# Top-k attention and two mixtures of experts on one core: the first replacement of the top-k search writes another buffer, and four smaller moves around it

## The chip, the cores and the metric

The kernel runs on one core of one Trainium2 chip. The metric is the device time of one execution in microseconds; given is the median of three runs. One more execution was taken with the hardware profiler, and all rows of a trace below are from that one. TensorE (PE) multiplies, PEld is its loading of weights; VectorE is DVE, ScalarE is ACT, GpSimd is POOL, and SyncE (SP) issues the DMAs.

## The reference, cut to what matters

```python
# attention: 4 batches, 8 heads, 576 tokens, 64 wide
scores = scale * np.matmul(q, k.transpose(0, 1, 3, 2))
kth = np.partition(scores, -32, axis=-1)[..., -32:-31]
scores = np.where(scores >= kth, scores, -1e9)
attn = np.exp(scores - np.max(scores, axis=-1, keepdims=True))
attn = attn / (np.sum(attn, axis=-1, keepdims=True) + 1e-09)
x = np.matmul(attn, v)                      # then [2304, 512]
# first MoE: w1, w2 [512, 1024], w3 [1024, 1024], w_out [1024, 512]
x = ((x @ w1) * (x @ w2)) @ w3 @ w_out
# second MoE: 8 experts, [512, 1024] and [1024, 512], a gate normalized 8 times
out = sum(P[:, e:e + 1] * (np.maximum(x @ m1[e], 0) @ m2[e]) for e in range(8))
```

## The kernel before

The first stage is a loop over 72 attention steps (and six more that drain it). A step holds two tiles of 128 query rows by 576 keys, `s_sb[st]` (128 x 2 x 576). The work of a step is spread over three turns of the loop. In turn s, VectorE searches the 32nd largest score of step s (`st_topk`), ScalarE marks and exponentiates step s−1 (`st_over`, `st_exp`), GpSimd scales step s−2 by the reciprocal of its sums (`st_norm`), TensorE transposes step s−2 (`st_trans`) and multiplies it with v (`st_av`), and TensorE already makes the scores of step s+1 (`st_scores`), which ScalarE evicts (L203).

The search: VectorE takes the larger of each pair of scores, half against half (`top`, L231). GpSimd has added the halves (`low`, L223) and subtracts `top` from that (L236), so `low` holds the smaller ones. In `rounds`, VectorE finds the eight largest (L242, MAX8) and overwrites them (L248, a MATCH_VALUE_LOAD and a MATCH_REPLACE8), four rounds in `top` and two in `low`, each for both tiles. Then L254 and L255 merge them. `head` is called between the first two maxima and issues the reciprocal (L282, VectorE), the two marks (L261, ScalarE), nbias (L266, GpSimd) and the two scalings (L288, GpSimd); GpSimd's L236 stand behind these in its queue.

Beside this, steps 0 to 23 convert four weights. A 'cv' takes a slab of 128 x 512 words of eight bytes (`raw`, L352), casts its parts with three instructions of ScalarE (L380, L381, L383, the last one in place), clamps on VectorE (`c1`, L390) and adds on GpSimd (L393, or L396 and then a split into two halves, L363 and L364). `c1` waits in the list `dve_q`; `rounds` takes one entry from it at every `dve_slot()`, that is behind each pair of maxima and each pair of replacements. `run_cv` starts at most two cvs a step. `cv_next` issues the load of a later cv. w3's slabs are transposed (L460), copied to `w3t` (L461) and multiplied with w_out into `W` (L469, L471). w1 and w2 are kept as two halves each. From step 24 on, `run_fill` places the products of the first MoE (L510, L528) between the attention's, a budget per step, so that a batch is done by a given step.

The order on every engine is the order in which this code is written; nothing is reordered later. Behind the loop come the rest of the last batch and the second MoE.

Of the kernel before, what the change touches and what calls it, by code (L numbers as in the profile page):

```python
# [18 lines left out]
def kernel(  # L19
# [163 lines left out]
    tkv, nbias, rden = {}, {}, {}  # L183
    eps = const.tile([128, 1], F32, name="eps")
    nc.gpsimd.memset(eps, 1e-9)

    def st_scores(st, j):
        p, h, t = steps1[st][j]
        ps = aps.tile([128, 2, 512], F32, name="sps", tag="sps")
        qs = qst_t[p % 2]  # L190
        if h is None:
            terms = [(qs[:, 2 * S4 + 128 * hh:2 * S4 + 128 * hh + 128], hh, part)
                     for part in range(2) for hh in range(2)]
        else:
            c0 = S4 * h + 128 * t
            terms = [(qs[:, c0:c0 + 128], h, part) for part in range(2)]
        for n, (lhs, hh, part) in enumerate(terms):
# [106 lines left out]
    def st_av(st):  # L304
# [6 lines left out]
        if steps1[st][0][1] is None:  # L311
# [8 lines left out]
            for j in range(2):  # L320
                b, hp = divmod(steps1[st][j][0], HP)
                nc.scalar.activation(xT[b][:, hp, S4:S], ps[:, 64 * j:64 * j + 64], AF.Copy)
            return
# [19 lines left out]
    gsc = G.rearrange("p f t -> p (f t)")  # L343
    cbias = const.tile([128, 2], F32, name="cbias")
    nc.gpsimd.memset(cbias[:, 0:1], -8.0 * 16 * 896)
    nc.gpsimd.memset(cbias[:, 1:2], -8.0 * (16 * 896 + 32768 - 4096))
    nc.gpsimd.memset(gsc[:, 0:2 * CW], 0.0)

    def cv_load(key, src):
        t = cv["p"].tile([128, 4 * CW + 4], U16, name="raw", tag="raw",  # L350
                         bufs=RB - 1 if "w2" in m1p else RB)
        nc.sync.dma_start(t[:, 1:4 * CW + 1], src.bitcast(U16))  # L352
        raws[key] = t

    def cv_next(pos):
        n = pos + (RB if pos < NCA else RB - 1)
        if n < len(cvs) and not pos < NCA <= n:
            cvs[n][1]()
# [11 lines left out]
    def cv_run(key, dst, done=None):  # L370
# [8 lines left out]
        cb = cv["p"].tile([128, CW], F32, name="cb", tag="cb", bufs=2)  # L379
        nc.scalar.activation(ca, y, AF.Relu, bias=cbias[:, 0:1], scale=8.0)  # L380
        nc.scalar.activation(cb, y, AF.Identity, bias=cbias[:, 1:2], scale=8.0)  # L381
        low = rest.bitcast(I32)
        nc.scalar.activation(low, rest, AF.Copy, scale=2.0 ** -13)  # L383

        def split():
            hi_lo(rest.bitcast(F32), *dst())
            cv_next(pos)

        def c1():
            nc.vector.scalar_tensor_tensor(Q.bitcast(U16).rearrange("p (n f) -> p n f", f=2)[:, :, 1],  # L390
                                           ca, 32768.0, cb, op0=ALU.min, op1=ALU.max)
            if key[0] in ("o", "3"):
                nc.gpsimd.tensor_tensor(dst().bitcast(I32), Q.bitcast(I32), low, ALU.add)  # L393
                cv_next(pos)
            else:
# [4 lines left out]

        dve_q.append(c1)

# [52 lines left out]
    def w_trans(i, hf):  # L455
        if hf == 0:
            w3t[i] = wtp.tile([128, FC, 128], F32, name="w3t", tag="w3t", bufs=1)
# [3 lines left out]
        nc.scalar.activation(w3t[i][:, 4 * hf:4 * hf + 4].rearrange("p a b -> p (a b)"), pt, AF.Copy)  # L461
        w3done.add((i, hf))
# [3 lines left out]
    def w_mm(i, j):  # L466
        if j == 0:
            wps[i] = mps.tile([128, 512], F32, name="wps", tag="mm")
        nc.tensor.matmul(wps[i], w3t[i][:, j], wo[:, j], start=(j == 0), stop=(j == FC - 1))  # L469
        if j == FC - 1:  # L470
            nc.scalar.activation(W[:, i], wps.pop(i), AF.Copy)  # L471

    def w_items(i, hf):
        return [(430, lambda: w_trans(i, hf))] + [(860, lambda j=j: w_mm(i, j)) for j in range(4 * hf, 4 * hf + 4)]

# [98 lines left out]
    def run_cv():  # L574
        n = cpos[0]
        if n >= len(cvs) or len(dve_q) > 1:
            return
# [3 lines left out]
        if n == NCA and "w2" not in m1p:  # L581
            if dve_q or cv_post or fill or later_q or (FC - 1, 1) not in w3done:
                return
            wt_close()
            for i in range(RB - 1):
                cvs[n + i][1]()
# [9 lines left out]
    cvs[0][1]()  # L596
    nc.scalar.activation(eps, eps, AF.Copy)
    prep_split(0, "k", nc.vector)
# [10 lines left out]
    cvs[1][1]()  # L609
    cvs[2][1]()  # L610
    load_v(1)
# [21 lines left out]
    for s in range(NS + 6):  # L633
        for fn in loads.get(s, []):
            fn()
        now[0] = s
        if s >= marks[0] and "p" not in m1p and cpos[0] == len(cvs) and not dve_q and not cv_post:
            moe1_pool()
# [45 lines left out]
        if old:  # L684
            st_trans(s - 2, 1)
        if 0 < s and cpos[0] < len(cvs):
            run_cv()
        cv_flush()
        some_prep(1)
# [376 lines left out]
```

## Time and profile before

| | us |
|---|---|
| three runs | 2574.52, 2576.54, 2577.63 |
| median | 2576.54 |
| the profiled execution | 2578.23 |
| its span, from the first to the last instruction | 2576.5 |
| TensorE busy in it | 2328.4 (90%) |
| VectorE busy | 1889.8 (73%) |
| GpSimd busy | 1568.2 (61%) |
| ScalarE busy | 1278.3 (50%) |

The shares are averages over stages with different limits, so they do not tell what a change in one stage is worth; the busy times by stretch do. A time in a row is microseconds from the span's start. Square brackets behind a row hold the idle time of that engine just before it and what ended it. The clock is the one granted to TensorE, as a share of its full speed. An engine's idle time costs something only where another one waits for it.

### The profile page before, as it was taken

To read this page: it belongs to the slowest core of one execution; us is meant where nothing else is said; L and a number is where in the kernel's file an instruction comes from. 1 tells how busy PE (TensorE), PEld (TensorE's weight loads), DVE (VectorE), ACT (ScalarE), POOL (GpSimd) and SP (SyncE) were. 2 spreads that over 40 slices of the span, in tenths; PEclk is the share of its full clock that TensorE was granted. 3 is DMA by queue.
4 is the path that set the end of the run, shared out by engine and by line. 5 is a ranking of instruction groups with operands and counts; after the bars stand their busy time and mean duration, and the time that the engine had idled before them with its cause. 6 is when DMAs were issued, how large, how long until landed. Compare 5 with 4: busy or idle time off the path is not lost.

```text
span 2576.5 us, 38951 instructions
## 1 busy us (share of the span) xinstructions
PE 2328.4 (90%) x13061; PEld 2028.4 (79%) x13061; DVE 1889.8 (73%) x4352; ACT 1278.3 (50%) x2757; POOL 1568.2 (61%) x1657
## 2 busy tenths in 40 slices
PE   4577669978878889999999999999999999999999
PEld 3444458867767768788999998888888899999998
DVE  6756777878777743688777777877777777777776
ACT  6667667666666643344444344434434444434432
POOL 5555666555655431568666667766666666666664
PEclk7788769999989999999999999999999999999999
DMA  4322211111111012322222223222222232222222
GB/s 128 102 71 81 64 53 33 38 38 35 29 41 30 8 40 73 98 70 78 66 66 71 69 66 107 72 68 66 66 66 69 71 91 66 69 72 66 66 66 58
DMA packets 173305, 166.66 MB, mean 65 GB/s; under 512 B 19632, under 2 KB 137392, under 8 KB 173104
## 3 DMA queue, kind: packets, MB, share of 16 engines
q1 hardware_dynamic: 173104, 164.17, 21.6%
q8 instruction: 103, 1.69, 0.3%
q14 instruction: 98, 0.80, 0.1%
HBM read 145.24 MB, written 9.44 MB: 60 GB/s over the span
## 4 chain that ended last, share of the span: by engine, by line
PE 61%; DVE 20%; POOL 7%; ACT 5%; issue 2%; DMA 2%; SPq 0%; POOLq 0%; ACTq 0%; DVEq 0%
PE y L953 29%; PE l1ps L886 25%; DVE tkv L242 8%; DVE top L248 4%; POOL low L236 3%; POOL e_sb L288 3%; PE abps L510 2%; DVE low L248 2%; PE x2ps L528 2%; DVE top L231 1%; DMA raw<-in_moe_w_dram 1%; PE wps L469 1%; ACT e_sb L273 1%; ACT G L380 1%; ACT s_sb L203 1%
## 5 line engine op out<-in xcount | busy, mean ns | idle before, releaser
L750 POOL TENSOR_TENSOR wal<-ws,wah 128x256 fp32r<-128x256 f32 x665 | 555.5, 843 | 480.5 <-ACT wah L749 471.0
L966 DVE SCALAR_TENSOR_TENSOR acc<-y,P,acc 128x512 f32<-128x512 f32 x540 | 402.6, 746 | 219.7 <-PE y L953 218.8
L749 ACT ACTIVATE wah<-ws 128x256 fp32r<-128x256 f32 x672 | 276.4, 413 | 525.9 <-PE l1ps L886 519.0
L953 PE MATMUL y<-wbh,hh 128*128 128x512 f32 x1152 | 457.1, 397 | 4.9 <-ACT hh L907 4.8
L953 PE MATMUL y<-wbl,hh 128*128 128x512 f32 x1152 | 455.2, 395 | 0.0
L953 PE MATMUL y<-wbh,hl 128*128 128x512 f32 x1152 | 449.7, 390 | 1.1 <-DVE hl L910 0.6
L743 DVE TENSOR_TENSOR ws<-ws 128x256 f32<-128x256 f32 x384 | 314.1, 819 | 3.9 <-DMA ws<-in_moe_w_dram 2.7
L886 PE MATMUL l1ps<-xo0h,wah 128*128 128x384 f32 x896 | 304.2, 340 | 0.0
L886 PE MATMUL l1ps<-xo0h,wal 128*128 128x384 f32 x896 | 302.5, 338 | 0.0
L886 PE MATMUL l1ps<-xo0l,wah 128*128 128x384 f32 x896 | 302.3, 337 | 0.0
L953 PEld LDWEIGHTS y<-wbl,hh 128*128 128x128 f32 x1152 | 216.5, 188 | 52.8
L907 ACT ACTIVATE hh<-u 128x384 fp32r<-128x384 f32 x192 | 100.9, 525 | 295.6 <-DVE u L899 295.6
L953 PEld LDWEIGHTS y<-wbh,hh 128*128 128x128 f32 x1152 | 216.9, 188 | 29.9 <-ACT hh L907 7.2
L758 POOL TENSOR_TENSOR wbl<-ws,wbh 128x1024 fp32r<-128x1024 f32 x96 | 232.0, 2416 | 12.6 <-ACT wbh L757 4.6
L953 PEld LDWEIGHTS y<-wbh,hl 128*128 128x128 f32 x1152 | 217.0, 188 | 28.4 <-DVE hl L910 3.9
L242 DVE MAX8 tkv<-top 128x8 f32<-128x288 f32 x576 | 237.9, 447 | 0.0
L294 PE MATMUL tps<-ident,e_sb 128*128 128x128 f32 x576 | 107.7, 318 | 122.6 <-POOL e_sb L288 113.2
L294 PEld LDWEIGHTS tps<-ident,e_sb 128*128 128x128 f32 x576 | 77.7, 163 | 161.6 <-POOL e_sb L288 131.0
L248 DVE MATCH_REPLACE8 top<-tkv,top 128x288 f32<-128x288 f32 x432 | 189.2, 443 | 0.0
L199 PE MATMUL sps<-kst,qst 128*128 128x288 f32 x640 | 143.9, 358 | 47.4 <-ACT s_sb L203 46.7
L886 PEld LDWEIGHTS l1ps<-xo0l,wah 128*128 128x128 f32 x896 | 169.1, 189 | 16.4
L886 PEld LDWEIGHTS l1ps<-xo0h,wah 128*128 128x128 f32 x896 | 168.7, 188 | 15.8 <-DVE u L899 0.6
(148 smaller groups left out, 5311.4 us busy)
## 6 DMA issues: line engine op xcount, KB each, us to landing
ws<-in_moe_w_dram SPq DMA_DIRECT2D x384, 128.0 KB, 2.4
ws<-in_moe_w_dram SPq DMA_DIRECT2D x96, 512.0 KB, 3.5
raw<-in_moe_w_dram SPq DMA_DIRECT2D x32, 512.0 KB, 4.0
kst<-kst SPq DMA_DIRECT2D x30, 288.0 KB, 4.1
xr<-x2s SPq DMA_DIRECT2D x12, 384.0 KB, 3.7
xr<-x2s SPq DMA_DIRECT2D x6, 768.0 KB, 4.6
kn<-in_k_dram SPq DMA_DIRECT2D x16, 256.0 KB, 2.9
qn<-in_q_dram SPq DMA_DIRECT2D x16, 256.0 KB, 2.9
```

What stands on the lines that cost most here:

```text
L199: nc.tensor.matmul(ps[:, e, 0:SH], lhs, kst[p, part][:, hh, SH * e:SH * e + SH], start=(n == 0), stop=(n == len(terms) - 1))
L242: nc.vector.max(vt[:, j, c0 + 8 * r:c0 + 8 * r + 8], x[:, j])
L248: nc.vector.match_replace(x[:, j], vt[:, j, c0 + 8 * r:c0 + 8 * r + 8], x[:, j], -3.0e38)
L294: nc.tensor.transpose(ps[:, 128 * c:128 * c + 128], e[:, 128 * c:128 * c + 128], ident)
L743: nc.vector.tensor_tensor(st[:, dst], st[:, x], st[:, y], op)
L749: nc.scalar.activation(hi, st[:, slot], AF.Copy)
L750: eng.tensor_tensor(lo, st[:, slot], hi.bitcast(F32), ALU.subtract)
L758: nc.gpsimd.tensor_tensor(lo, st, hi.bitcast(F32), ALU.subtract)
L886: nc.tensor.matmul(ps[:, 0:TH], lhs[:, c], rhs[:, slot, c], start=(k_ == 0), stop=(k_ == 3 * KH - 1))
L907: nc.scalar.activation(t["hh"][:, i, h], src, AF.Relu)
L953: nc.tensor.matmul(ps, lhs[:, m, h, o:o + 128], rhs[:, m], start=(k_ == 0), stop=(k_ == 5))
L966: nc.vector.scalar_tensor_tensor(a, ps, P[:, t, e:e + 1], a, op0=ALU.mult, op1=ALU.add)
```

## The change

Five things are done.

1. `st_topk` has a second tile, `rest`. The first pair of replacements reads `top` and writes `rest`; all later rounds of that search work in `rest`. `top` is no longer written after L231 (L230 in the new numbering).
2. `e_sb` is `s_sb`: the exponentials overwrite the scores. `s_sb` has four buffers in place of three, `e_sb`'s two are gone. The sum's 1e-9 is added by VectorE just ahead of the reciprocal, and no longer by ScalarE (L276).
3. The third cast writes to words of its own, to a part of G or to the tile `lw` in turn; `raw` is then free behind the three casts, two of them are kept (three before), and `cv_next` is called right there. `c1` is put into `dve_q` behind two empty entries.
4. The eviction of x (L331, L322) is put off to the next turn of the loop, behind the first exponential.
5. The four products of a half of w3 are put off until the next half has been transposed; `w3t` is two half tiles.

```diff
-            s_sb[st] = ap1.tile([128, 2, S], F32, name="s_sb", tag="s_sb", bufs=3)
+            s_sb[st] = ap1.tile([128, 2, S], F32, name="s_sb", tag="s_sb", bufs=4)
...
+        rest = ap1.tile([128, 2, SH], F32, name="rest", tag="rest", bufs=1)
...
-        def rounds(x, c0, k):
+        def rounds(x, c0, k, y=None):
...
-                        nc.vector.match_replace(x[:, j], vt[:, j, c0 + 8 * r:c0 + 8 * r + 8], x[:, j], -3.0e38)
+                        nc.vector.match_replace((x if y is None else y)[:, j], vt[:, j, c0 + 8 * r:c0 + 8 * r + 8],
+                                                x[:, j], -3.0e38)
+                    x = x if y is None else y
...
-        rounds(top, 0, TOPK // 8)
+        rounds(top, 0, TOPK // 8, rest)
...
-            e_sb[st] = ap1.tile([128, 2, S], F32, name="e_sb", tag="e_sb", bufs=2)
+            e_sb[st] = s_sb[st]
...
-            nc.scalar.activation(rd, rd, AF.Identity, bias=eps)
...
+        nc.vector.tensor_scalar(rd, rd, 1e-9, None, op0=ALU.add)
         nc.vector.reciprocal(rd, rd)
...
-        nc.scalar.activation(xT[b][:, hp, 128 * t:128 * t + 128], ps[:, 0:128], AF.Copy)
+        xev.append(lambda: nc.scalar.activation(xT[b][:, hp, 128 * t:128 * t + 128], ps[:, 0:128], AF.Copy))
...
-    RB = 3
+    RB = 2
...
-        nc.scalar.activation(cb, y, AF.Identity, bias=cbias[:, 1:2], scale=8.0)
-        low = rest.bitcast(I32)
+        low = (cv["p"].tile([128, CW], F32, name="lw", tag="lw", bufs=1) if n else gsc[:, 4 * CW:5 * CW]).bitcast(I32)
+        nc.scalar.activation(ca, y, AF.Relu, bias=cbias, scale=8.0)
+        nc.scalar.activation(cb, y, AF.Copy, bias=-8.0 * (16 * 896 + 32768 - 4096), scale=8.0)
         nc.scalar.activation(low, rest, AF.Copy, scale=2.0 ** -13)
+        cv_next(pos)
...
-        dve_q.append(c1)
+        dve_q.extend([None, None, c1])
...
+        r = [(430, lambda: w_trans(i, hf))] + w_last
+        w_last[:] = [(860, lambda j=j: w_mm(i, j)) for j in range(4 * hf, 4 * hf + 4)]
...
             st_exp(s - 1, 0)
+        st_out()
```

The order on VectorE in one of the steps with two cvs, before: `top` is the tile of the larger scores, `tkv` the maxima found, L390 the clamp of a cv.

```order
L231 TENSOR_TENSOR top<-s_sb 128x288 x2
L242 MAX tkv<-top 128x8
L282 RECIPROCAL rden<-rden 128x2
L242 MAX tkv<-top 128x8
L390 SCALAR_TENSOR_TENSOR G<-G,cb 128x512
L248 MATCH_REPLACE top<-tkv,top 128x288 x2
L390 SCALAR_TENSOR_TENSOR G<-G,cb 128x512
L242 MAX tkv<-top 128x8 x2
L248 MATCH_REPLACE top<-tkv,top 128x288 x2
```

And the same place of the changed program (the clamp is L397 there):

```order
L230 TENSOR_TENSOR top<-s_sb 128x288 x2
L241 MAX tkv<-top 128x8
L282 TENSOR_SCALAR rden<-rden 128x2
L283 RECIPROCAL rden<-rden 128x2
L241 MAX tkv<-top 128x8
L247 MATCH_REPLACE rest<-tkv,top 128x288 x2
L241 MAX tkv<-rest 128x8 x2
L397 SCALAR_TENSOR_TENSOR G<-G,cb 128x512
L247 MATCH_REPLACE rest<-tkv,rest 128x288 x2
L241 MAX tkv<-rest 128x8 x2
L247 MATCH_REPLACE rest<-tkv,rest 128x288 x2
L397 SCALAR_TENSOR_TENSOR G<-G,cb 128x512
```

The first replacement no longer writes what it reads; the two clamps moved from the first and second slot of the step to the third and sixth; one small instruction stands ahead of the reciprocal.

On ScalarE, the end of such a step and the start of the next, before: L297 evicts transposes, three casts of a cv, w3's copy, x, three casts of the second cv, and then the next step's marks and scores.

```order
L297 ACTIVATE et<-tps 128x640
L380 ACTIVATE G<-raw,cbias 128x512
L381 ACTIVATE cb<-raw,cbias 128x512
L383 ACTIVATE raw<-raw 128x512
L461 ACTIVATE w3t<-pt 128x512
L331 ACTIVATE xT<-xps 128x128
L380 ACTIVATE G<-raw,cbias 128x512
L381 ACTIVATE cb<-raw,cbias 128x512
L383 ACTIVATE raw<-raw 128x512
L261 ACTIVATE s_sb<-s_sb,tkv 128x576 x2
L203 ACTIVATE s_sb<-sps 128x576
```

And the same place of the changed program:

```order
L388 ACTIVATE G<-raw,cbias 128x512
L389 ACTIVATE cb<-raw 128x512
L390 ACTIVATE lw<-raw 128x512
L476 ACTIVATE W<-wps 128x512
L466 ACTIVATE w3t<-pt 128x512
L388 ACTIVATE G<-raw,cbias 128x512
L389 ACTIVATE cb<-raw 128x512
L390 ACTIVATE G<-raw 128x512
L262 ACTIVATE s_sb<-s_sb,tkv 128x576 x2
L201 ACTIVATE s_sb<-sps 128x576
L274 ACTIVATE s_sb,rden<-s_sb,nbias 128x576
L333 ACTIVATE xT<-xps 128x128
```

The eviction of x moved from ahead of the second cv's casts to behind the next step's first exponential, and the third cast writes `lw` or G in place of `raw`.

## Rows read from the trace of the kernel before

**Rows 1.** Stretches: from:to, length; busy PE, PEld, DVE, ACT, POOL; clock, DMA share, GB/s
```profile
14.13:81.70 67.57, 31.84 (x178) 26.22 (x178) 54.87 (x173) 50.54 (x96) 42.58 (x45) 0.67 0.44 132
81.70:280.24 198.54, 142.31 (x741) 88.93 (x741) 130.31 (x421) 134.50 (x266) 109.38 (x121) 0.83 0.25 76
280.24:374.97 94.73, 53.78 (x312) 43.27 (x313) 74.28 (x241) 65.31 (x129) 61.24 (x68) 0.68 0.22 67
374.97:526.35 151.38, 138.28 (x1099) 121.98 (x1097) 120.14 (x431) 100.90 (x226) 87.73 (x114) 1.00 0.14 38
526.35:934.20 407.85, 336.24 (x2543) 295.78 (x2543) 323.79 (x1157) 257.61 (x563) 222.21 (x293) 0.93 0.10 27
934.20:2576.40 1642.20, 1620.82 (x8169) 1447.87 (x8169) 1183.77 (x1932) 664.25 (x1470) 1042.47 (x1002) 1.00 0.24 72
```

**Rows 2.** Waits of VectorE in stretches A to E: us in total, times, longest
```profile
DVE top L248 <- POOL low L236: 5.4, 8, 1.4
DVE G L390 <- ACT cb L381: 5.0, 2, 4.8
...
DVE top L248 <- POOL low L236: 38.2, 24, 5.3
DVE G L390 <- ACT cb L381: 23.2, 12, 4.6
...
DVE top L248 <- POOL low L236: 12.7, 11, 2.8
DVE G L390 <- ACT cb L381: 7.2, 4, 2.7
...
DVE top L248 <- POOL low L236: 30.4, 26, 2.4
...
DVE top L248 <- POOL low L236: 81.3, 70, 2.4
```

**Rows 3.** Timeline of step 52, VectorE and GpSimd: start, length, engine, line, instruction
```profile
700.68 0.82 DVE L231 TENSOR_TENSOR top<-s_sb 128x288 f32<-128x288 f32 x2
...
700.84 0.34 POOL L266 TENSOR_TENSOR nbias<-tkv 128x2 f32<-128x2 f32 x1 [4.04 <-DVE tkv L255]
...
701.78 0.15 DVE L282 RECIPROCAL rden<-rden 128x2 f32<-128x2 f32 x1
701.85 0.44 DVE L242 MAX8 tkv<-top 128x8 f32<-128x288 f32 x1
702.10 1.47 POOL L288 TENSOR_SCALAR e_sb<-e_sb,rden 128x576 f32<-128x576 f32 x2 [0.92 <-DVE rden L282]
...
703.54 1.56 POOL L236 TENSOR_TENSOR low<-low,top 128x288 int32<-128x288 int32 x2
...
704.37 0.09 DVE L248 MATCH_VALUE_LOAD top<-tkv,top 128x8 f32 x1 [2.09 <-POOL low L236]
...
705.57 0.81 DVE L242 MAX8 tkv<-top 128x8 f32<-128x288 f32 x2
...
709.44 0.80 DVE L242 MAX8 tkv<-low 128x8 f32<-128x288 f32 x2
...
712.19 0.45 DVE L231 TENSOR_TENSOR top<-s_sb 128x288 f32<-128x288 f32 x1
```

**Rows 4.** Waits: TensorE and ScalarE in stretch B, then TensorE in E
```profile
PE wps L469 <- ACT w3t L461: 41.9, 15, 7.0
...
ACT xT L331 <- PE xps L327: 20.1, 5, 5.7
ACT G L380 <- DMA raw<-in_moe_w_dram: 15.4, 4, 4.6
...
PE tps L294 <- POOL e_sb L288: 64.3, 33, 4.9
```

**Rows 5.** Durations in ns, min/median/max: the clamp, and a small tensor_scalar
```profile
L390 DVE SCALAR_TENSOR_TENSOR G<-G,cb x40: 710/754/1615, 18.0 to 354.4; 128x512 uint16<-128x512 f32 x40
...
L859 DVE TENSOR_SCALAR cs<-cs x8: 171/373/2044, 1073.8 to 1130.0; 128x8 f32<-128x8 f32 x8
```

More of the change, by code (lines that the diff above doesn't have):

```diff
@@ L183 @@
     tkv, nbias, rden = {}, {}, {}
-    eps = const.tile([128, 1], F32, name="eps")
-    nc.gpsimd.memset(eps, 1e-9)
     def st_scores(st, j):
@@ L321, in st_av @@
                 b, hp = divmod(steps1[st][j][0], HP)
-                nc.scalar.activation(xT[b][:, hp, S4:S], ps[:, 64 * j:64 * j + 64], AF.Copy)
+                xev.append(lambda b=b, hp=hp, j=j: nc.scalar.activation(xT[b][:, hp, S4:S], ps[:, 64 * j:64 * j + 64],
+                                                                        AF.Copy))
             return
@@ L330, in st_av, with st_out @@
         b, hp = divmod(p, HP)
-        nc.scalar.activation(xT[b][:, hp, 128 * t:128 * t + 128], ps[:, 0:128], AF.Copy)
+        xev.append(lambda: nc.scalar.activation(xT[b][:, hp, 128 * t:128 * t + 128], ps[:, 0:128], AF.Copy))
+    xev = []
+    def st_out():
+        while xev:
+            xev.pop(0)()
     CW = 512
-    RB = 3
+    RB = 2
     wt = ExitStack()
@@ L343 @@
     gsc = G.rearrange("p f t -> p (f t)")
-    cbias = const.tile([128, 2], F32, name="cbias")
-    nc.gpsimd.memset(cbias[:, 0:1], -8.0 * 16 * 896)
-    nc.gpsimd.memset(cbias[:, 1:2], -8.0 * (16 * 896 + 32768 - 4096))
+    cbias = const.tile([128, 1], F32, name="cbias")
+    nc.gpsimd.memset(cbias, -8.0 * 16 * 896)
     nc.gpsimd.memset(gsc[:, 0:2 * CW], 0.0)
@@ L350, in cv_load @@
         t = cv["p"].tile([128, 4 * CW + 4], U16, name="raw", tag="raw",
-                         bufs=RB - 1 if "w2" in m1p else RB)
+                         bufs=RB)
         nc.sync.dma_start(t[:, 1:4 * CW + 1], src.bitcast(U16))
@@ L355, in cv_next @@
     def cv_next(pos):
-        n = pos + (RB if pos < NCA else RB - 1)
+        n = pos + RB
         if n < len(cvs) and not pos < NCA <= n:
@@ L379, in cv_run @@
         cb = cv["p"].tile([128, CW], F32, name="cb", tag="cb", bufs=2)
-        nc.scalar.activation(ca, y, AF.Relu, bias=cbias[:, 0:1], scale=8.0)
-        nc.scalar.activation(cb, y, AF.Identity, bias=cbias[:, 1:2], scale=8.0)
-        low = rest.bitcast(I32)
+        low = (cv["p"].tile([128, CW], F32, name="lw", tag="lw", bufs=1) if n else gsc[:, 4 * CW:5 * CW]).bitcast(I32)
+        nc.scalar.activation(ca, y, AF.Relu, bias=cbias, scale=8.0)
+        nc.scalar.activation(cb, y, AF.Copy, bias=-8.0 * (16 * 896 + 32768 - 4096), scale=8.0)
         nc.scalar.activation(low, rest, AF.Copy, scale=2.0 ** -13)
+        cv_next(pos)
         def split():
-            hi_lo(rest.bitcast(F32), *dst())
-            cv_next(pos)
+            hi_lo(low.bitcast(F32), *dst())
         def c1():
@@ L393, in c1 @@
                 nc.gpsimd.tensor_tensor(dst().bitcast(I32), Q.bitcast(I32), low, ALU.add)
-                cv_next(pos)
             else:
@@ L455, in w_trans @@
     def w_trans(i, hf):
-        if hf == 0:
-            w3t[i] = wtp.tile([128, FC, 128], F32, name="w3t", tag="w3t", bufs=1)
+        w3t[i, hf] = wtp.tile([128, 4, 128], F32, name="w3t", tag="w3t", bufs=2)
         pt = mps.tile([128, 512], F32, name="pt", tag="mm")
@@ L460, in w_trans @@
             nc.tensor.transpose(pt[:, 128 * j:128 * j + 128], w3r[i, hf][:, 128 * j:128 * j + 128], ident)
-        nc.scalar.activation(w3t[i][:, 4 * hf:4 * hf + 4].rearrange("p a b -> p (a b)"), pt, AF.Copy)
+        nc.scalar.activation(w3t[i, hf].rearrange("p a b -> p (a b)"), pt, AF.Copy)
         w3done.add((i, hf))
@@ L468, in w_mm @@
             wps[i] = mps.tile([128, 512], F32, name="wps", tag="mm")
-        nc.tensor.matmul(wps[i], w3t[i][:, j], wo[:, j], start=(j == 0), stop=(j == FC - 1))
+        nc.tensor.matmul(wps[i], w3t[i, j // 4][:, j % 4], wo[:, j], start=(j == 0), stop=(j == FC - 1))
         if j == FC - 1:
             nc.scalar.activation(W[:, i], wps.pop(i), AF.Copy)
+    w_last = []
     def w_items(i, hf):
-        return [(430, lambda: w_trans(i, hf))] + [(860, lambda j=j: w_mm(i, j)) for j in range(4 * hf, 4 * hf + 4)]
+        r = [(430, lambda: w_trans(i, hf))] + w_last
+        w_last[:] = [(860, lambda j=j: w_mm(i, j)) for j in range(4 * hf, 4 * hf + 4)]
+        if (i, hf) == (FC - 1, 1):
+            r += w_last
+        return r
     def moe1_pool():
@@ L575, in run_cv @@
         n = cpos[0]
-        if n >= len(cvs) or len(dve_q) > 1:
+        if n >= len(cvs) or len(dve_q) > 3:
             return
@@ L581, in run_cv @@
         if n == NCA and "w2" not in m1p:
-            if dve_q or cv_post or fill or later_q or (FC - 1, 1) not in w3done:
+            if any(dve_q) or cv_post or fill or later_q or (FC - 1, 1) not in w3done:
                 return
             wt_close()
-            for i in range(RB - 1):
+            for i in range(RB):
                 cvs[n + i][1]()
@@ L596 @@
     cvs[0][1]()
-    nc.scalar.activation(eps, eps, AF.Copy)
+    nc.scalar.activation(cbias, cbias, AF.Copy)
     prep_split(0, "k", nc.vector)
@@ L609 @@
     cvs[1][1]()
-    cvs[2][1]()
     load_v(1)
@@ L636 @@
         now[0] = s
-        if s >= marks[0] and "p" not in m1p and cpos[0] == len(cvs) and not dve_q and not cv_post:
+        if s >= marks[0] and "p" not in m1p and cpos[0] == len(cvs) and not any(dve_q) and not cv_post:
             moe1_pool()
@@ L685 @@
             st_trans(s - 2, 1)
+        cv_flush()
         if 0 < s and cpos[0] < len(cvs):
             run_cv()
-        cv_flush()
         some_prep(1)
```

## The prediction

> **What bounds the kernel now.** I read the stretch table first [rows 1]. Behind 934.20 TensorE is busy for 1620.82 of 1642.20 us at a granted clock of 1.00. That is the mixture of experts and its lead-in, the change touches nothing there, and it can only begin earlier. Everything to be won lies in the 72 attention steps between 14.13 and 934.20, which I cut into five stretches: A (steps 0 to 4), B (5 to 16: w3 and w1 are converted and W is multiplied), C (17 to 23: w2 is converted), D (24 to 36: TensorE carries the first batch's gated products) and E (37 to 71). The edges are starts of steps, taken from the first L231 of each.
>
> Next, what VectorE waits for in each stretch [rows 2]. In D and E it waits for one thing only: the first replacement of a step (L248) for GpSimd's subtraction (L236), 30.4 us in 13 steps and 81.3 us in 35, so 2.3 us a step. One step shows why [rows 3]. L236 reads `top` and L248 overwrites it. GpSimd's queue runs nbias, the two scalings L288 (which start after the reciprocal at 701.78) and then the two L236 from 703.54. VectorE is through with the second maximum at about 702.2 (701.85 and the 0.36 that one of the pair at 705.57 takes) and its replacement starts at 704.37, after 2.09 us of idleness; with the second replacement's own wait (70 waits in 35 steps) it is 2.32 us a step. `low` itself is wanted only at 709.44. The step is 11.51 us long (700.68 to 712.19).
>
> In B and C there is a second wait, L390 for the cast L381 (23.2 and 7.2 us). Behind it stands a ring: ScalarE's casts are queued behind the eviction of x (L331), which waits 20.1 us for TensorE, and TensorE waits 41.9 us for ScalarE's copy of w3's transposes (L461); the casts also wait 15.4 us for raw words [rows 4].
>
> **The change part by part.** Every sum below is made against the profiled execution, 2578.23 us for a span of 2576.5; the median of the three runs is 2576.54, so 1.7 us come off at the end.
>
> *First replacement into `rest`.* Nothing is added in number; six replacements a step stay six. L247 then reads `top` and GpSimd's subtraction may read it at the same time. What is late next is the first maximum of `low`, which does need the subtraction. In the step shown, GpSimd ends it near 705.1; VectorE would be there at 709.44 − 2.32 + 0.2, or 707.3 (the 0.2 is the next item). That leaves 2 us, so the wait goes and does not move.
>
> *eps by VectorE.* ScalarE loses L276, which no engine waits for in D and E. VectorE gains one tensor_scalar on 128x2 between the first two maxima. The nearest row is L859, 128x8 of the same form: 0.171 us at least, 2.044 us at most [rows 5]. I take 0.2 us a step, since the reciprocal must now follow it, because in [rows 3] GpSimd idles from the end of nbias at 701.18 to 702.10, just when it would run. The upper end, 1.9 us more, is a rival below. The Trainium skill, page "SBUF — State Buffer", section "Who interferes with whom", has a rule that speaks against this edit: such an instruction takes a port pair shared with GpSimd and, if GpSimd came first, blocks until that instruction ends. The spread of L859 agrees with it; were GpSimd always in the way, the sum by that rule would lose up to 135 us (72 x 1.87), where the rows of step 52 make it 14.
>
> *Exponentials over the scores, four buffers.* e_sb's two buffers go, s_sb gets a fourth. The new tile of step s+1 overwrites that of step s−3, whose last reader is TensorE's transpose in step s−1. TensorE has that behind it before it multiplies the scores that are to be evicted, so I cost this at nothing; it would cost only with TensorE more than half a step behind.
>
> *Raw words end with the casts; the product three slots later.* `low` gets words of its own (a piece of G and a tile `lw`), so the next-but-one load is issued after the three casts instead of after GpSimd's last use. The 15.4 us for raw words in B go, since a load then has about a whole step. L397 stands behind the second pair of maxima and behind the third pair of replacements: the 23.2 and 7.2 us should go too. Against it: it now meets GpSimd's scalings and subtractions. L390 took 0.710 at least, 0.754 in the median and 1.615 us at most [rows 5]; I take 0.2 us more for each of the 40, 8 us in all; the ends are 0 and 0.86 us each. And `lw` has one buffer: in steps that convert w1 or w2, the third cast waits until GpSimd has made the low half of the word before it, which is queued behind the later product. Those are ScalarE's new waits, and its later casts and the next step's first activations stand behind them.
>
> *x evicted, w3's products a step later.* xT's eviction then finds TensorE long done, and w3's products find their transposes copied. That takes apart the ring: 20.1 us of ScalarE and 41.9 us of TensorE in B [rows 4]. No instruction is added; the last product of W comes one step later, and so does the closing of the pool (step 17), while the opening for the gated products stays at step 23.
>
> **The sum by stretch**, from [rows 1, 2]. The new length is the largest of what the engines then need.
> - E: VectorE 407.85 − 81.3 + 35 x 0.2 = 333.6. TensorE is busy 336.24 at clock 0.93 and would need about 308 at 1.00 (0.07 x 407.85 less). In this stretch it waits 64.3 us for GpSimd's scaling [rows 4], and those waits shrink with the step. I take 336: 72 less.
> - D: VectorE 151.38 − 30.4 + 2.6 = 123.6; TensorE is busy 138.28 at clock 1.00 and becomes the bound. I take 139: 12 less.
> - C: VectorE 94.73 − 12.7 − 7.2 + 1.4 = 76.2, and 1.6 for eight slower products. Every word here is split into two halves and every other one lies in `lw`; I take 80: 15 less. The upper end is 85, with the wait for the cast left where it is.
> - B: VectorE 198.54 − 38.2 − 23.2 + 2.4 = 139.5, and 4.6 for 23 slower products; TensorE is busy 142.31 (clock 0.83), ScalarE 134.50. Three engines that hand work to each other and are all nearly full do not fit into the largest of them; I take 150, as near to the largest as D is loose today (151.38 against 138.28, some 9%, of which I leave half): 48 less. The ends are 142 (TensorE as busy as now and never waiting) and 167 (198.54 − 38.2 + 2.4 + 4.6, the wait for the cast left where it is).
> - A: 67.57 − 5.4, about 1.6 of the 5.0 us for the first cast (two pairs more go ahead of it), and 2.8 back for eps (five steps) and nine slower products: 4 less.
>
> Together 72 + 12 + 15 + 48 + 4 = 151 us: 2578.2 − 151 − 1.7, that is 2425 us, 5.9% less. What lies behind 934.20 is costed at nothing: it is TensorE's own work.
>
> **The rivals.**
> 1. *TensorE is the bound nearly everywhere and its clock stays low.* In B, C and E the clock was 0.83, 0.68 and 0.93. For: its busy time there is only a few us under my sums. Against: in D, where it waits least, the clock was 1.00. Price: if E keeps a fifth of TensorE's 64.3 us of waiting, B half of the 41.9, and D 4 us, 13 + 13 + 4 come back: 2455.
> 2. *GpSimd's queue sets B and C.* The later product holds up L223, the splits and the next step's nbias behind it, and ScalarE waits on `lw`. At the upper ends of both, 17 + 5 us are lost; if eps also meets GpSimd and costs 0.7 us a step in place of 0.2, 36 more: 2447 to 2483.
> 3. *The wait moves to the first maximum of `low`.* This decides if GpSimd's subtraction ends more than 2 us later in the step than now, because low's sums, the gated products and the splits of the step before still fill its queue when nbias comes. Then every step stays 11.5 us and pays eps besides: 72 x 0.2, plus 14 us: 2591, slower. Against: GpSimd is busy 222.21 of 407.85 us in E, and would be at two thirds in 336.
> 4. *The change does not do what it says:* some other wait of the first replacement on GpSimd remains. In the order of the changed program that instruction waits for nothing of another engine; 2577.
> 5. *All cover holds.* B reaches 140, C 76, E 326 (the 1.2 us between the first load at 704.37 and the next maximum at 705.57 shrink as well): 2400.
>
> **How the numbers follow.** The forecast with 5 (2390 to 2447) has 0.66, rivals 1 and 2 together 0.26 (2447 to 2490), rival 3 0.05, rival 4 0.03. A measurement of this kernel can tell about 0.2% (5 us) from no change. Faster: 0.92. Same: 0.03. Slower: 0.05. The range goes from 2390 to 2480 and leaves out the far end of rival 2 and what goes beyond it, and 3 and 4.
>
> **What would show it.** Right: L247 with no wait for GpSimd and step lengths near 9.4 us in E, 10.6 in D, about 12.5 in B; no wait of TensorE for w3t, none of ScalarE for x or for raw words; PEclk at or near full behind step 24. Wrong: a wait of L241 for `low` near 2 us (rival 3), tensor_scalar L282 far over 0.2 us, TensorE busy over 97% in E at a clock under 0.95 (rival 1), or ScalarE waiting on GpSimd before L390 for more than 30 us in B and C (rival 2).

## The result: 2418.95 us, and the profile after

The changed kernel takes 2418.95 us in the median of four runs (2418.12 to 2419.59); the kernel before, run beside it on the same chip, took 2575.98 us (2574.52 to 2577.63). The ratio is 0.939, with a 95% interval from 0.9374 to 0.9406. The forecast was 2425 us.

The view that answers to [rows 1] comes first: the busy times by stretch of the kernel after, cut at the same steps (a row: from:to, length; busy time of PE, PEld, DVE, ACT and POOL with the number of instructions; clock, DMA share, GB/s).

```profile
14.07:74.61 60.54, 32.53 (x178) 26.77 (x178) 55.93 (x175) 47.96 (x91) 41.83 (x45) 0.86 0.48 143
74.61:215.59 140.98, 121.95 (x735) 78.25 (x736) 139.75 (x432) 126.95 (x253) 110.24 (x121) 0.94 0.34 105
215.59:294.57 78.98, 46.38 (x310) 37.34 (x308) 78.26 (x247) 63.12 (x123) 62.77 (x69) 0.81 0.29 87
294.57:428.53 133.96, 133.09 (x1083) 120.58 (x1082) 130.12 (x444) 94.91 (x212) 87.49 (x114) 1.00 0.15 40
...
428.53:768.87 340.34, 316.80 (x2571) 281.33 (x2568) 336.74 (x1192) 242.43 (x528) 222.18 (x291) 0.98 0.12 34
768.87:2417.80 1648.93, 1627.93 (x8174) 1451.49 (x8172) 1188.09 (x1935) 666.83 (x1470) 1041.43 (x1003) 1.00 0.24 71
```

E ends here with the last merge of a search (L256), which in the kernel before lies at 933.81 and not at the 934.20 of [rows 1]; before's E is 407.46 us long by this cut, and the rest 1642.65. VectorE is busy for 139.75 of 140.98 us in B, 78.26 of 78.98 in C and 336.74 of 340.34 in E: it now sets the pace nearly everywhere. In D TensorE does, 133.09 of 133.96 us.

| stretch | before, us | after, us | difference | forecast |
|---|---|---|---|---|
| A | 67.57 | 60.54 | −7.0 | −4 |
| B | 198.54 | 140.98 | −57.6 | −48 |
| C | 94.73 | 78.98 | −15.8 | −15 |
| D | 151.38 | 133.96 | −17.4 | −12 |
| E | 407.46 | 340.34 | −67.1 | −72 |
| the rest | 1642.65 | 1648.93 | +6.3 | 0 |

The waits over all 72 steps of the kernel after, VectorE's first, then the two longest of TensorE and those of ScalarE for `lw` and raw words, answer to [rows 2, 4] (a row: engine, what waits <- whom it waits for: us in total, times, longest).

```profile
DVE top L230 <- ACT s_sb L201: 4.1, 2, 2.3
DVE tkv L241 <- POOL low L235: 2.5, 5, 0.9
DVE G L397 <- ACT cb L389: 1.9, 1, 1.9
...
PE tps L295 <- POOL s_sb L289: 55.9, 22, 6.4
PE sps L197 <- ACT s_sb L201: 17.6, 11, 7.4
...
ACT lw L390 <- POOL w1l L371: 10.4, 5, 4.2
...
ACT lw L390 <- POOL w2l L371: 5.9, 3, 4.1
...
ACT G L388 <- DMA raw<-in_moe_w_out_dram: 4.3, 1, 4.3
```

The first replacement (L247) waits for nobody any more; the 168.0 us in the five L248 rows of [rows 2] became 2.5 us before the first maximum of `low` (L241). TensorE no longer waits for `w3t`, and what is left of the waits for raw words lies in the first steps. Step 45 answers to [rows 3] (timeline: start, length, engine, line, instruction).

```profile
509.03 0.82 DVE L230 TENSOR_TENSOR top<-s_sb 128x288 f32<-128x288 f32 x2
...
510.13 0.15 DVE L282 TENSOR_SCALAR rden<-rden 128x2 f32<-128x2 f32 x1
...
510.40 0.44 DVE L241 MAX8 tkv<-top 128x8 f32<-128x288 f32 x1
...
510.75 0.07 DVE L247 MATCH_VALUE_LOAD rest<-tkv,top 128x8 f32 x1
...
511.60 0.81 DVE L241 MAX8 tkv<-rest 128x8 f32<-128x288 f32 x2
512.02 1.56 POOL L235 TENSOR_TENSOR low<-low,top 128x288 int32<-128x288 int32 x2
...
515.47 0.81 DVE L241 MAX8 tkv<-low 128x8 f32<-128x288 f32 x2
...
518.22 0.82 DVE L230 TENSOR_TENSOR top<-s_sb 128x288 f32<-128x288 f32 x2
```

GpSimd's subtraction starts at 512.02, when VectorE is already at its second round, and ends at 513.58; `low` is wanted at 515.47, 1.9 us later. The step is 9.19 us long (509.03 to 518.22), and 9.19 to 9.20 us is what 14 of the 35 steps of E take.

### The profile page after: what moved, and what is told of

Read it like the earlier page. It is cut to its first block, busy times and chain, and to the rows that moved or that the text cites. A ratio compares the mean times of both kernels' runs of the same rounds, so it can differ in the third digit from the quotient of the medians.

```text
span 2417.8 us, 38838 instructions
## 1 busy us (share of the span) xinstructions
PE 2283.8 (94%) x13061; PEld 2000.1 (83%) x13061; DVE 1931.5 (80%) x4424; ACT 1247.4 (52%) x2685; POOL 1568.5 (65%) x1655
## 4 chain that ended last, share of the span: by engine, by line
PE 68%; DVE 26%; ACT 2%; POOL 2%; issue 1%; DMA 1%; SPq 0%; POOLq 0%; ACTq 0%
PE y L964 32%; PE l1ps L897 28%; DVE tkv L241 10%; DVE rest L247 6%; PE abps L521 4%; DVE top L230 3%; PE x2ps L539 2%; DVE low L247 2%; DVE G L397 1%; DVE tkv L255 1%; DMA xr<-x2s 1%; PE tps L295 1%; PE xps L329 1%; DVE rden L282 0%; PE sps L197 0%
## 5 line engine op out<-in xcount | busy, mean ns | idle before, releaser
L964 PE MATMUL y<-wbh,hl 128*128 128x512 f32 x1152 | 455.3, 395 | 2.0 <-DVE hl L921 1.6
L964 PE MATMUL y<-wbh,hh 128*128 128x512 f32 x1152 | 452.1, 392 | 2.8 <-ACT hh L918 2.8
L241 DVE MAX8 tkv<-rest 128x8 f32<-128x288 f32 x432 | 175.1, 447 | 0.0
L897 PEld LDWEIGHTS l1ps<-xo0h,wal 128*128 128x128 f32 x896 | 169.2, 189 | 0.0
L295 PE MATMUL tps<-ident,s_sb 128*128 128x128 f32 x576 | 97.6, 296 | 70.5 <-POOL s_sb L289 55.9
L910 DVE TENSOR_TENSOR u<-l1ps,u 128x384 f32<-128x384 f32 x288 | 157.3, 546 | 4.1 <-PE l1ps L897 3.1
L921 DVE SCALAR_TENSOR_TENSOR hl<-u,hh 128x384 fp32r<-128x384 f32 x192 | 111.6, 581 | 57.2 <-ACT hh L918 57.2
```

What stands on the lines that cost most here:

```text
L295: nc.tensor.transpose(ps[:, 128 * c:128 * c + 128], e[:, 128 * c:128 * c + 128], ident)
L897: nc.tensor.matmul(ps[:, 0:TH], lhs[:, c], rhs[:, slot, c], start=(k_ == 0), stop=(k_ == 3 * KH - 1))
L910: nc.vector.tensor_tensor(t[nm], ps, t[x], ALU.add)
L921: nc.vector.scalar_tensor_tensor(t["hl"][:, i, h], src, 0.0, t["hh"][:, i, h].bitcast(F32), op0=ALU.max, op1=ALU.subtract)
L964: nc.tensor.matmul(ps, lhs[:, m, h, o:o + 128], rhs[:, m], start=(k_ == 0), stop=(k_ == 5))
```

## The experiments

Each ran beside the kernel before on the same chip, and its ratio is to that. Those that start from the kernel after say so. A difference to the kernel after is one of medians from two chips, on which the kernel before takes 2572.97 to 2575.98 us, so up to 3 us of such a difference can be the chip's.

**The first two edits alone.** The kernel before with `rest`, and with the exponentials over the scores in four buffers (that makes the room for `rest`). Raw words, clamps, x and w3's products stay as they were.

```diff
...
-        rounds(top, 0, TOPK // 8)
+        rounds(top, 0, TOPK // 8, rest)
...
-            e_sb[st] = ap1.tile([128, 2, S], F32, name="e_sb", tag="e_sb", bufs=2)
+            e_sb[st] = s_sb[st]
```

> The kernel before with two edits alone: the first replacement writes rest, and the exponentials overwrite the scores in four buffers (that makes the room); eps stays on ScalarE, and casts, loads, x and w3's products stand as before. Theory (every wait is worth its own length): D and E shorten as in the changed kernel, B by its 38 us of waiting for GpSimd's subtraction and C by its 13; 2425 to 2440. Rival (the ring of ScalarE and TensorE binds in B and C, and VectorE's wait for the cast grows by what the other one loses): B stays above 180 and C above 90, 2455 to 2475.

Measured: 2475.14 us, ratio 0.9619 (0.9605 to 0.9634). Its stretches B to E, then B's waits of VectorE, TensorE and ScalarE:

```profile
75.94:270.08 194.14, 138.88 (x713) 87.09 (x713) 129.05 (x420) 133.52 (x264) 105.13 (x117) 0.83 0.24 78
270.08:360.44 90.36, 52.96 (x316) 41.43 (x317) 75.64 (x241) 67.74 (x134) 66.37 (x72) 0.68 0.23 71
360.44:494.54 134.10, 133.56 (x1081) 121.82 (x1078) 124.07 (x430) 98.36 (x222) 86.79 (x113) 0.99 0.13 37
494.54:834.15 339.61, 319.31 (x2584) 284.71 (x2582) 330.11 (x1157) 256.64 (x569) 224.23 (x292) 0.97 0.13 35
```

```profile
DVE G L393 <- ACT cb L384: 53.4, 13, 8.0
...
PE wps L472 <- ACT w3t L464: 41.9, 14, 7.0
...
ACT xT L334 <- PE xps L330: 19.4, 5, 5.0
ACT G L383 <- DMA raw<-in_moe_w_dram: 17.2, 5, 4.5
```

D and E have their whole gain from these two edits (134.10 and 339.61 us). B gives only 4.4 us and C the same: in B VectorE's wait for GpSimd is gone, but its wait for the cast has grown from 23.2 us [rows 2] to 53.4. The ring of [rows 4] sets B's length, and a wait taken out of it lengthens the next.

**The other edits alone**: the kernel after, with the replacement in place again.

```diff
-        rounds(top, 0, TOPK // 8, rest)
+        rounds(top, 0, TOPK // 8)
```

> The changed kernel with the first replacement in place again; all else as changed. Theory: VectorE waits for the subtraction in every step again, 2.3 us in D and E and as much or more in B and C, less what GpSimd then no longer holds up; about 2540 to 2560. Rival (the waits of B and C came from the ring and stay away): 2500 to 2525.

Measured: 2556.41 us, ratio 0.9935 (0.9921 to 0.995). Stretches B and E, and VectorE's wait in each:

```profile
81.27:246.27 165.00, 131.79 (x741) 82.89 (x741) 136.81 (x432) 128.43 (x253) 104.77 (x121) 0.89 0.28 88
494.55:906.54 411.99, 335.49 (x2543) 295.28 (x2543) 328.71 (x1192) 244.13 (x527) 221.29 (x291) 0.93 0.10 27
```

```profile
DVE top L247 <- POOL low L235: 27.0, 24, 2.1
...
DVE top L247 <- POOL low L235: 79.7, 70, 2.1
```

E is 412 us again, and VectorE waits in it for nothing but the subtraction. B is 165.0, C 95.0, D 153.3. So the two halves of the change are worth 98 us (the first experiment) and 17 us alone, and 157 together. The surplus lies in B and C, where each half leaves the other's wait standing and only both open the stretch: B is 194.1 and 165.0 alone and 140.98 together, C 90.4 and 95.0 alone and 78.98 together.

**w3's products right behind their transposes**, from the kernel after:

```diff
-        r = [(430, lambda: w_trans(i, hf))] + w_last
-        w_last[:] = [(860, lambda j=j: w_mm(i, j)) for j in range(4 * hf, 4 * hf + 4)]
...
+        return [(430, lambda: w_trans(i, hf))] + [(860, lambda j=j: w_mm(i, j)) for j in range(4 * hf, 4 * hf + 4)]
```

> The changed kernel with one part undone: w3's products follow their own transposes again. Theory: TensorE, busy 122 of B's 141 us, waits some 40 us for ScalarE's copy again and becomes the bound: B 15 to 25 us longer; 2434 to 2444. Rival (TensorE's wait is spent out of its slack): B longer by under 8 us, 2418 to 2427.

Measured: 2446.72 us, ratio 0.9501 (0.9487 to 0.9515), 28 us more than the kernel after, all of it in B (169.48 us). VectorE's and TensorE's waits there:

```profile
DVE top L230 <- ACT s_sb L201: 18.1, 7, 4.9
DVE G L397 <- ACT cb L389: 13.1, 5, 7.0
...
PE wps L474 <- ACT w3t L466: 38.6, 14, 4.9
```

TensorE's wait for the copies is back at 38.6 us (41.9 before), and VectorE, which waits for nobody in B of the kernel after, waits 31.2 us for ScalarE behind it. That accounts for B's 28.5 us, which is more than the 15 to 25 expected.

**Raw words as before**, from the kernel after: the third cast in place, the load behind GpSimd's last use, three buffers.

```diff
-    RB = 2
+    RB = 3
...
-        low = (cv["p"].tile([128, CW], F32, name="lw", tag="lw", bufs=1) if n else gsc[:, 4 * CW:5 * CW]).bitcast(I32)
+        low = rest.bitcast(I32)
...
-        cv_next(pos)
```

> The changed kernel with one part undone: the third cast works in place in raw, three raw buffers, and the next load is issued behind GpSimd's last use. Theory: ScalarE waits for raw words again, some 15 us in B and 19 in C, and in front of its casts; 2435 to 2450. Rival (the loads are covered by the later clamp; in their place ScalarE's 16 us of waiting for lw go): 2412 to 2422.

Measured: 2439.37 us, ratio 0.9471 (0.9457 to 0.9485), 20 us more than after: B 148.19, C 90.23. In C, VectorE's wait and ScalarE's:

```profile
DVE G L397 <- ACT cb L389: 13.8, 4, 6.0
...
ACT G L388 <- DMA raw<-in_moe_w_dram: 17.5, 6, 5.6
```

The casts wait for words that were asked for too late, and the clamp for the casts. In C the raw words as they were cost 11.3 of the 15.8 us that C had won.

**The clamp's slot, and the eviction of x**, two runs from the kernel after, each with one edit undone:

```diff
-        dve_q.extend([None, None, c1])
+        dve_q.append(c1)
...
-        if n >= len(cvs) or len(dve_q) > 3:
+        if n >= len(cvs) or len(dve_q) > 1:
```

> The changed kernel with one part undone: the clamp of a cv goes back to the first and second slot of the step (behind the first maxima and the first replacements). Theory (the later slot is what gives the casts time): VectorE waits for the second cv's casts again in B and C, 15 to 30 us; 2434 to 2449. Rival (the casts come early enough since x and w3's products are out of their way, and a later slot only costs meetings with GpSimd): B and C within 5 us of the changed kernel, 2412 to 2424.

```diff
             st_exp(s - 1, 0)
-        st_out()
...
+            st_out()
```

> The changed kernel with one part undone: x is evicted at the end of its own step again, ahead of the second cv's casts. Theory: ScalarE waits about 20 us in B for TensorE, and since it is 90% busy there, half of it or more reaches VectorE: B 10 to 20 us longer; 2429 to 2439. Rival (the later clamp covers it): 2416 to 2424.

Measured: 2420.73 us (0.94, 0.9386 to 0.9414) and 2419.47 us (0.9393, 0.9378 to 0.9409). Neither differs from the kernel after. With x evicted at the end of its step ScalarE does wait for TensorE, but only 2.5 us in B, and VectorE waits for nobody there. Each of these two edits has no price of its own once the others are in; both undone together were not run.

**Without the 1e-9**, from the kernel after. (The sum that it is added to holds a term of exp(0) = 1, so in 32-bit words nothing of it is left anyway.)

```diff
-        nc.vector.tensor_scalar(rd, rd, 1e-9, None, op0=ALU.add)
```

> The changed kernel without the addition of 1e-9 to the softmax's sum on any engine (the sum is at least 1, which 1e-9 does not change in float32). Theory: VectorE is the bound in all five stretches, so each of the 72 steps gives back the instruction's 0.2 us, and the 10 us go that it is held up by GpSimd; 2393 to 2400. Rival (TensorE is the bound in D and E): only A to C gain, 2410 to 2416.

Measured: 2407.37 us, ratio 0.9355 (0.934 to 0.9371), 11.6 us less than after. The undisturbed step is 8.99 us here and 9.19 there, so the instruction costs the 0.2 us a step that were forecast; D, which is TensorE's, doesn't get shorter (134.74 us). By the ratios, which take out the chip, the gain is 9 us, and the expectation held neither way: the total lies between the theory's range and the rival's. In the profiled executions A gives 0.8 us, B 4.4, C 1.3, E 5.2 and the rest 1.4, and D takes 0.8. E should have given 35 x 0.2 = 7.0 and 6.0 us more, by which the instruction was longer there than its shortest; a part of this came back in L230, which in the same sense is 13.1 us longer in E, in place of 7.5 (the next paragraph is about such times). VectorE's wait for `low` over all steps grew from 2.5 to

```profile
DVE tkv L241 <- POOL low L235: 10.9, 15, 3.4
```

of which 9.0 us lie in D, where TensorE sets the pace, and only 2.0 in E: there the margin before `low` still holds in most steps.

**Five attempts at what is left.** The step of 9.19 us isn't what E's mean is (9.72). Step 62 shows the difference (timeline, as above):

```profile
671.67 2.42 DVE L230 TENSOR_TENSOR top<-s_sb 128x288 f32<-128x288 f32 x2
672.12 1.65 POOL L128 TENSOR_TENSOR qhl<-qn,qhl 128x576 fp32r<-128x576 f32 x1
673.74 3.18 POOL L505 TENSOR_TENSOR xl<-xT,xh 128x1280 fp32r<-128x1280 f32 x1
...
674.38 2.56 DVE L282 TENSOR_SCALAR rden<-rden 128x2 f32<-128x2 f32 x1
676.88 0.19 POOL L267 TENSOR_TENSOR nbias<-tkv 128x2 f32<-128x2 f32 x1
...
684.88 0.45 DVE L230 TENSOR_TENSOR top<-s_sb 128x288 f32<-128x288 f32 x1
```

The pair L230 takes 2.42 us in place of 0.82 while GpSimd splits q (L128), and the small tensor_scalar, 0.15 us otherwise, takes 2.56 us and ends (676.94) when GpSimd's L505 does (676.92). Nothing waits in the sense of the view of waits: the instructions are longer. The step takes 13.21 us. I call the time of an instruction over the shortest of its kind its hold-up; summed over L230, L255, L282 and L397 it is 62.8 us in the kernel after and 21.5 us in the kernel before (over L231, L254 and L390). By the GpSimd instruction that overlaps the held one most, 22 of the 62.8 us lie beside the subtractions that make the low halves of k and q, and 7 beside that of x.

GpSimd's long subtractions in pieces, so that a held instruction waits for a piece (k and q in three, x in four):

```diff
-        eng.tensor_tensor(hl[:, :, 1, :], src, hl[:, :, 0, :].bitcast(F32), ALU.subtract)
+        for c in range(0, 2 * R + 1, 3):
+            eng.tensor_tensor(hl[:, c:c + 3, 1, :], src[:, c:c + 3], hl[:, c:c + 3, 0, :].bitcast(F32), ALU.subtract)
...
-            eng.tensor_tensor(xl[:, c:c + step, 0:n], x, xh[:, c:c + step, 0:n].bitcast(F32), ALU.subtract)
+            for d in range(c, c + step):
+                eng.tensor_tensor(xl[:, d, 0:n], xT[b][:, d, t0:t1], xh[:, d, 0:n].bitcast(F32), ALU.subtract)
```

> The changed kernel with GpSimd's long subtractions cut: the low halves of k and q in three instructions in place of one, those of x in four. The arithmetic is the same. Theory: VectorE's two-input instructions at a step's edge and the addition of eps wait until the GpSimd instruction in progress has ended; 22 us of their 63 us of lengthening fall on the subtractions of k and q and 7 on that of x, and two thirds of it go: 2398 to 2405. Rival (GpSimd only falls behind by the extra instructions, or VectorE is held up by the next piece): 2415 to 2422.

Measured: 2414.88 us, ratio 0.9385 (0.9371 to 0.9399): 4 us less than after (1 us by the ratios), a difference smaller than the interval. The hold-ups fell to 48.7 us. The split of k a step earlier:

```diff
-        for fn in ops[:2]:
-            prep.setdefault(max(f0, 0), []).append(fn)
+        prep.setdefault(max(f0 - 1, 0), []).insert(0, ops[0])
+        prep.setdefault(max(f0, 0), []).append(ops[1])
```

> The changed kernel with one thing moved: the split of k (L127 on ScalarE, L128 on GpSimd) is placed one step earlier and that of q stays, so no step carries both, and GpSimd is no longer in the second one when VectorE reaches the step's edge. No instruction is added or removed. Theory (VectorE is the bound and is held up by the GpSimd instruction it meets): of the 22 us that fall on these two subtractions at least half go; 2403 to 2410. Rival (VectorE then meets another GpSimd instruction, or the time goes to TensorE): 2416 to 2422.

Measured: 2419.01 us, ratio 0.9392 (0.9376 to 0.9408): no difference. The hold-ups are 59.8 us: 9 of the 22 us beside the two subtractions went, and most of that came up beside other instructions of GpSimd. No 1e-9, x in four pieces and the shift together:

> The changed kernel with three edits: no 1e-9 (it does not change a float32 sum of 1 or more), the split of k a step earlier, and x's low half in four instructions of GpSimd. Theory: their gains add up to nearly their sum, since all three shorten VectorE's own time; 2390 to 2398. Rival (TensorE is the bound by now, 134 us in D and 314 to 320 in E): no better than without the 1e-9 alone, 2402 to 2408.

Measured: 2407.12 us, ratio 0.9348 (0.9334 to 0.9362), the same as without the 1e-9 alone. Next, the work of GpSimd not moved but taken away:

```diff
-        eng.tensor_tensor(hl[:, :, 1, :], src, hl[:, :, 0, :].bitcast(F32), ALU.subtract)
+        if p == 0:
+            eng.tensor_tensor(hl[:, :, 1, :], src, hl[:, :, 0, :].bitcast(F32), ALU.subtract)
+        else:
+            nc.scalar.activation(hl[:, :, 1, :], src, AF.Copy, scale=2.0 ** -14)
```

> The kernel after, but behind the first pair of heads the low halves of k and q are not the true remainders: ScalarE writes a scaled copy of k or q in their place, and GpSimd no longer has the long subtractions that make them, so the scores are other numbers than the reference's. Theory: the time in which VectorE is held up by a GpSimd instruction in progress is a loss of its own; with these two subtractions gone the 20 us that lay beside them (qhl 14, khl 6) are not found again elsewhere, E gets 8 to 10 us shorter, B 4, C 2, D stays with TensorE: 2403 to 2410 us. Rival: as when the split of k was moved, the hold-ups reappear beside other GpSimd instructions, since GpSimd is busy two thirds of the time whatever it does: 2414 to 2420 us.

Measured: 2407.84 us, ratio 0.935 (0.9335 to 0.9366), 11.1 us less than after. The hold-ups fell by 23.4 us to 39.4, about as much as lay beside these subtractions, so this time they are not found again elsewhere. But only half of that reaches the end. Stretch E and VectorE's waits in it:

```profile
419.66:757.54 337.88, 316.51 (x2581) 280.37 (x2580) 329.02 (x1192) 249.94 (x542) 207.01 (x280) 0.99 0.13 35
```

```profile
DVE tkv L244 <- POOL low L238: 4.3, 6, 1.9
DVE top L233 <- ACT s_sb L204: 0.9, 2, 0.7
```

VectorE is busy 7.7 us less in E, and 5.2 us of that are new waits, for `low` and for the scores: E got 2.5 us shorter, not the 8 to 10 expected. The total came out as the theory said, since A, B and C gave 3.6, 4.5 and 1.8 us. There the hold-ups fell by 3.9, 4.5 and 1.9 us, so each microsecond of them came back; D's fell by 4.5, and D, which is TensorE's, got no shorter (134.9 us).

The fifth spreads TensorE's products of D into E, besides the pieces and the missing 1e-9:

```diff
...
+        if left and s + left == marks[1]:
+            left += 1.5
```

> The kernel after without the 1e-9 (left out of the attention's sums), with GpSimd's long subtractions cut in pieces (k and q in three, x in four), and with the first batch's gated products spread over one and a half steps more than the planner's due time, so that TensorE has less to do in each step of D. Theory: D, which is TensorE's (133 of 134 us), gets shorter, 126 to 128, E takes the products over at 3 us; with the 11.6 us of the missing 1e-9 that makes 2394 to 2402 us. Rival: what D gives, E takes, since VectorE's and TensorE's work there are both near the step's length: 2404 to 2408 us, no better than leaving the 1e-9 out alone.

Measured: 2412.28 us, ratio 0.9366 (0.9352 to 0.938), no better than without the 1e-9 alone (2407.37), and above both ranges expected. D and E, and VectorE's wait in E:

```profile
286.79:417.64 130.85, 126.72 (x1053) 116.36 (x1052) 122.08 (x430) 94.10 (x210) 88.77 (x129) 1.00 0.14 38
417.64:759.75 342.11, 322.62 (x2601) 286.22 (x2599) 328.01 (x1157) 243.14 (x531) 228.77 (x328) 0.98 0.13 34
```

```profile
DVE tkv L242 <- POOL low L236: 11.2, 15, 3.0
```

D gave 3.9 us against the run without the 1e-9 and E took 6.9: TensorE has 9 us more to do in E, and the wait for `low` in E is at 11.2 us, where it was 2.0. How much of that wait comes from the pieces, which the other run doesn't have, was not separated.

## Why the prediction was right, and where its sizes were off

**The mechanism held.** `rest` takes VectorE's wait out and doesn't move it: the margin of 2 us before the first maximum of `low` was measured at 1.9 us in step 45, and rival 3 needed more than that. The second experiment shows that without `rest` the 80 us of E stay; the first that D and E need nothing else. Rival 4 is out, since the wait is gone, and rival 1 too: in E TensorE is busy 93% at clock 0.98, where the rival needed over 97% at under 0.95.

**The step of E** was forecast at 9.4 us and is 9.19 us undisturbed. The 0.2 us for eps was right. What the forecast left standing are the gaps around the old wait: from the first load to the next maximum 1.20 us [rows 3], 0.85 after (510.75 to 511.60), that is 0.35 less, of which the second replacement's own wait explains 0.23; rival 5 had named this. And from the second maximum's start to that load's, without the wait, it was 0.43 us [rows 3] and is 0.35 (510.40 to 510.75). Together that is the 0.2 us.

**E came out 5 us over the forecast nevertheless** (67.1 won, not 72). 35 steps of 9.19 us are 321.7; L230, L255 and L282 are held up for another 7.5, 5.6 and 6.0 us in E, which makes 340.8 against 340.34 measured. In E of the kernel before the hold-ups of L231 and L254 were 0.9 and 3.8 us. The step that failed is the sum "407.85 − 81.3 + 35 x 0.2 = 333.6", which took all other work of VectorE at its old length. TensorE is not what sets E: busy 316.80 us, and waiting for GpSimd's scaling for 9.7.

**D** is TensorE's, as forecast, at clock 1.00; it was sized by a busy time of 138.28 us [rows 1], and that became 133.09 with 16 matmuls fewer recorded in the stretch and 28 more in E. The single products take as long as before (`xps`, 128x128: 278 ns in the mean both times). In the second experiment, which has the same order of products on TensorE but VectorE's old wait, D has 1104 records and E 2543; in the kernel after 1083 and 2571. The last product with v of a turn (L329) starts 2.3 to 4.3 us before VectorE's next step in D there, and from 0.5 us before to 2.2 us behind it in the kernel after. So TensorE falls behind VectorE in D and carries some of D's products over the edge into E. The sum had all of them end in D.

**B** was sized at 150 with an allowance for three full engines that hand work to each other; it came out at 140.98, where rival 5 had it. The allowance was the wrong term: with the ring open, the two other engines have room. TensorE's 142.31 us were taken at clock 0.83; it is now busy 121.95 us at 0.94 with six matmuls fewer. VectorE's own sum, 139.5 + 4.6, was 3 us too long.

**The ring** was read rightly, but of the four edits two carry its price. By the runs, in each of which one edit is undone, w3's products a step later are worth 28 us and the raw words 20 us; the eviction of x (20.1 us of waiting in [rows 4]) and the later slot of the clamp nothing. The prediction gave the clamp's waits to the slot ("the 23.2 and 7.2 us should go too"); by the runs they went with the two edits that let the casts come earlier: with either of these undone, a wait of 13 us for the cast is back (the two L397 rows above for B and C).

**The later clamp** was to cost 0.2 us each, 8 us in all, between 0 and 0.86 each. It costs nothing (the min, median and max of a duration, in ns, then the first and last start; this view answers to [rows 5]):

```profile
L397 DVE SCALAR_TENSOR_TENSOR G<-G,cb x40: 711/748/1161, 19.5 to 278.4; 128x512 uint16<-128x512 f32 x40
...
L282 DVE TENSOR_SCALAR rden<-rden x72: 143/149/2570, 41.3 to 772.6; 128x2 f32<-128x2 f32 x72
...
L230 DVE TENSOR_TENSOR top<-s_sb x144: 443/451/1697, 14.1 to 760.0; 128x288 f32<-128x288 f32 x144
...
L255 DVE TENSOR_TENSOR tkv<-tkv x72: 191/193/1347, 28.3 to 768.5; 128x32 f32<-128x32 f32 x72
...
L241 DVE MAX8 tkv<-rest x432: 429/446/464, 18.8 to 765.7; 128x8 f32<-128x288 f32 x144
```

**Eps and the shared port.** L282 was held up by more than 0.3 us 9 times in 72, three of these took more than 2.5 us, and it lost 10.3 us in all. So the bound of 135 us was far off, and 0.2 us a step, 14 us in all, was near the 9 to 12 that leaving it out gives back. The rule that was weighed there (the Trainium skill, page "SBUF — State Buffer", section "Who interferes with whom") is right on what happens in step 62, with 2.56 us beside L505; how often it happens only the order of GpSimd's work told. The same section says that a VectorE instruction with two inputs in SBUF contends with GpSimd's reads, and one with a single input outside the wide modes doesn't. The trace agrees: L230 (two inputs) reaches 1697 ns, L255 1347 ns, while the 432 L241 (one input) stay between 429 and 464 ns.

**ScalarE's new waits for `lw`** are there, 10.4 and 5.9 us, as rival 2 said, below its 30 us; VectorE waits for a cast once, for 1.9 us, in A. In B and C, where the waits for `lw` are, it waits for nobody.

**A** gave 7.0 us where 4 were forecast. **The rest** was costed at nothing and is 6.3 us longer. TensorE is busy 1627.93 us there in place of 1620.82, at clock 1.00, with the same products. The first experiment has 1641.4 us, the second 1648.0, so it comes with the edits that the first experiment leaves out; undone one at a time, the slot, x, w3's products and the raw words each leave it between 1646.9 and 1648.7, and without the 1e-9 it is 1647.5. Its cause stays open.

The errors add up to little because they go both ways: 9.6 us in B, 5.4 in D, 3.0 in A and 0.8 in C more than forecast, 4.9 in E and 6.3 in the rest less; 151 us forecast, 158.6 measured. That the total is only 6 us off is in part luck.

## What to carry to other kernels

Look for an instruction that writes what another engine still reads: a separate target for the first of a row of updates cost no instruction here and gave 98 us with the room that it needed. A ring of engines gives up its time only when all its links that bind are loosened, so price it by pairs of edits, not by adding the waits in it; of four links here two had a price when undone alone. And once an engine has no waits left, the lengths of its instructions beside those of an engine that holds it up are the next thing to read: the view of waits doesn't show them.

## What was not expected of the hardware

Taking VectorE's wait away made GpSimd hold it up for longer. The second experiment and the kernel after have the same instructions and differ only in where the first replacement writes: the hold-ups are 29.6 us there and 62.8 after. Between the kernel before and the first experiment they went from 21.5 to 42.0. The rows of before that answer to L230 and L255 above are these (durations as above); they have long instructions too, only fewer of them:

```profile
L231 DVE TENSOR_TENSOR top<-s_sb x144: 446/450/1552, 14.1 to 922.6; 128x288 f32<-128x288 f32 x144
...
L254 DVE TENSOR_TENSOR tkv<-tkv x72: 191/192/1979, 32.0 to 933.4; 128x32 f32<-128x32 f32 x72
```

GpSimd is busy 58% of the 72 steps in the second experiment and 69% in the kernel after, with nearly the same microseconds (514.5 and 524.5) in a shorter time, and of the 328 instructions of VectorE that are counted here 101 and 141 start while GpSimd is at work. Whether the denser work or the new order of the two within a step does more isn't shown. Cutting GpSimd's subtractions into pieces or moving one gave no time clear of the noise; only taking them away did (23.4 us of hold-ups, 11.1 us of time).
